# Turning the output products of a second MoE to features by tokens, and placing TensorE's operands at one offset modulo 512 bytes

## The chip, the core and the metric

The kernel runs on one core of one Trainium2 chip. The metric is the device time of one execution in microseconds (us); the median of the runs is given. Of the engines, PE is TensorE (PEld its weight loads), DVE is VectorE, ACT is ScalarE, POOL is GpSimd and SP is SyncE, which issues all transfers here.

## The reference

Three stages follow one another: linear attention with a decaying state, a gated MoE (one expert) with silu, and a second MoE (one expert) with g = h - tanh(h).

```python
for t in range(S):                                   # B, H, S, D = 4, 8, 768, 48
    cur = einsum('bhd,bhe->bhde', u * k[t], v[t])
    y[t] = einsum('bhd,bhde->bhe', r[t], state + cur)
    state = w[t][..., None] * state + einsum('bhd,bhe->bhde', k[t], v[t])
x = y as (3072 tokens, 384)
x = (silu(x @ w_gate) * (x @ w_val)) @ w_out         # d_ff 1536
h = x @ w_in                                         # d_ff 2048
return (h - tanh(h)) @ w_out2                        # (3072, 384)
```

## The kernel before

**Number format.** Activations and weights are split into a high part (rounded to fp32r) and a low part (the rest, also fp32r). Each product is three fp32r matmuls: high by high, high by low, low by high. The attention uses plain fp32 matmuls.

**Tiling.** The 3072 tokens are six blocks of TB = 512; the 384 features are KD = 3 chunks of 128. A matmul multiplies a stationary operand (128 x 128, loaded by a weight load ahead of it) with a moving one of up to 512 columns, into one PSUM bank.

**Order.** The order of the instructions is written by hand (`manual_schedule`), and each engine runs its own in program order.

1. Attention, in 24 units, is interleaved with the first half (f = 0 to 5) of the first MoE over the six blocks (`mlp`, L597): per f, nine projection matmuls for the gate, nine for the value (`proj`, L512, the matmul is L516), and nine output products (`po`, L644). The output products have the weights stationary and the 512 tokens moving, into three PSUM banks a0 to a2 (features by tokens). Attention's own matmuls are L267, L287, L304, L347 and L354.
2. Attention's pools are closed and wpb is opened in their place. The second half (f = 6 to 11) runs over the six blocks alone, one step of 27 matmuls per f. Its weights are in wpb.
3. The second MoE: per block j and m = 0 to 15 (`hm`, L835) nine projection matmuls into a bank from `ptile`; `act1` (L840) then makes z and zs on ACT, t and g on DVE and the high part hi on ACT; `act2` (L851) makes the low part lo one step later on DVE. `om` (L870) runs two steps after its `hm`: it calls `oprod` (L861), which has a slice of 128 tokens of g stationary and the 384 columns of the weight moving, for four token slices, three matmuls each (L867), into four banks. After m = 15 the four banks are copied out (L879 on DVE, L881 on ACT) and stored by SP (L883). One step is thus hm(m), then om(m - 2).
4. At the end, small sums on DVE decide (two flags) whether slow fallback paths run; for these inputs they don't.

**The second MoE's weights.** W2 has 32 tiles: the first 18 (m = 0 to 8) go to wpa, the others (m = 9 to 15) to wpb.

**Where the tiles lie.** In each SBUF partition, pools follow one another in the order in which they are opened, each tile rounded up to 32 bytes. Most tiles are multiples of 512 bytes; a few small ones shift what comes behind them. Worked out from the sizes, the byte offset modulo 512 is:

| pool, tiles | before |
|---|---|
| wpa (weights), xp (x, x2), sb (s, t, hi, lo) | 96 |
| mx, okf, fs, fi at the end of sb (32 bytes each) | 96 to 192 |
| f64, stage, ws, wpb (weights) | 224 |
| attention io: four w of 2080 bytes, then rk, rkd, v | 224 to 320, then 352 |
| attention wk: ident, cm; then rst, wmx; then SE, kT | 352; then 416 |
| attention wk: four P of 2080, e, x0; then c; then kt, A, q | then 32; then 96 |

The slices that a matmul takes are 512 bytes apart (v: 256), so they keep their tile's offset.

Of the kernel before, what the change touches and what calls it, by code (L numbers as in the profile page):

```python
# [8 lines left out]
FP32 = mybir.dt.float32  # L9
FP32R = mybir.dt.float32r  # L10
I32 = mybir.dt.int32
# [7 lines left out]
NTOK, DM = B * S, H * D  # L19
HR = 64  # L20
FF1, FF2 = 1536, 2048
NF, NM = FF1 // 128, FF2 // 128
KD = DM // 128
TB = 512
NB = NTOK // TB
HF = NF // 2
CW = 129
# [86 lines left out]
class attention:  # L114
# [3 lines left out]
    def __init__(self, nc, ctx, tc, const, ins, accw, accx):  # L118
        self.nc = nc
        self.rkw_d, self.tok_d, self.v_d, self.ub_d = ins  # L120
        self.accw, self.accx = accw, accx
        self.const = const
        PSUM = bass.MemoryType.PSUM
        self.io = ctx.enter_context(tc.tile_pool(name="io", bufs=3))
        self.wk = ctx.enter_context(tc.tile_pool(name="wk", bufs=2))
        self.ps = ctx.enter_context(tc.tile_pool(name="aps", bufs=3, space=PSUM))
        self.u = [dict() for _ in range(NU)]
        wk = self.wk
        self.u_sb = wk.tile([128, 2, 2 * 96], FP32, name="u_sb", bufs=1)
        self.ident = wk.tile([128, 128], FP32, name="ident", bufs=1)  # L130
        self.cm = wk.tile([128, 4, 128], U32, name="cm", bufs=1)
        self.rst = wk.tile([128, 4, CW], FP32, name="rst", bufs=1)
        self.wmx = wk.tile([128, 1], FP32, name="wmx", bufs=1)

        self.SE = [[[wk.tile([128, 2, 128], FP32, name=f"SE{a}{b}{c}", bufs=1) for c in range(2)]
                    for b in range(2)] for a in range(2)]
# [22 lines left out]
    def load_w(self, u):  # L159
        if u >= NU:  # L160
            return
        s = self.u[u]
        s["w"] = self.io.tile([128, 4 * CW], FP32, tag="w", name="w", bufs=4)
        self.nc.sync.dma_start(out=s["w"], in_=self.rkw_d[u, :, 1024:])

    def load_rk(self, u):
# [26 lines left out]
    def scan(self, u):  # L193
        s = self.u[u]
        w = s["w"]
        s["P"] = self.wk.tile([128, 4, CW], FP32, tag="P", name="P", bufs=4)
        fl = lambda x: x.rearrange("p a b -> p (a b)")
        self.nc.vector.tensor_tensor_scan(fl(s["P"]), w, fl(self.rst), 0.0, ALU.mult, ALU.max)  # L198
        yield
# [20 lines left out]
    def diag(self, u):  # L220
        nc, s = self.nc, self.u[u]
        r, k = s["rk"][:, 0, :], s["rk"][:, 1, :]
        nc.vector.tensor_tensor(r, r, k, ALU.mult)
        yield
        r4 = r.rearrange("p (a c e) -> p a c e", a=2, c=2)
        ub = self.u_sb[:, u % 2, :].rearrange("p (a e) -> p a e", a=2)
        nc.vector.tensor_tensor(r4, r4, ub[:, :, None, :].to_broadcast([128, 2, 2, 96]), ALU.mult)
        yield
        s["c"] = self.wk.tile([128, 8], FP32, tag="c", name="c")
        nc.vector.tensor_reduce(s["c"], r.rearrange("p (c d) -> p c d", d=D), AX.X, ALU.add)  # L230
        yield

# [243 lines left out]
def body(ctx: ExitStack, tc: tile.TileContext, rkw, tok, vtok, ub, w1, w2, rf, kf, vf, wf, uf, out):  # L476
    nc = tc.nc
    PSUM = bass.MemoryType.PSUM

    const = ctx.enter_context(tc.tile_pool(name="const", bufs=1))  # L480
# [15 lines left out]
    sa_t = const.tile([128, 1], FP32, name="sa_t")  # L496
    qa_t = const.tile([128, 1], FP32, name="qa_t")
    zsw_t = const.tile([128, 1], FP32, name="zsw_t")
    xs_d = dram.tile([NB, 128, 2, KD, TB], FP32, name="xs_d")
    pt_d = dram.tile([NB, 128, KD, TB], FP32, name="pt_d")  # L500
    w_d = dram.tile([3 * NF + 2 * NM, 128, 2, 384], FP32, name="w_d")
# [152 lines left out]
    with tc.manual_schedule():  # L654
# [53 lines left out]
        for b in range(NB):  # L708
            last = b == NB - 1
            if last:  # L710
                cb.until(3 * HF)
                pa.close()
                ex = ctx.enter_context(tc.tile_pool(name="ex", bufs=2, space=PSUM))
                wpb = ctx.enter_context(tc.tile_pool(name="wpb", bufs=3 * HF))
                pb = ExitStack()
                pin = pb.enter_context(tc.tile_pool(name="pin", bufs=2))
                x2p = pb.enter_context(tc.tile_pool(name="x2p", bufs=1))
                for i in cb.order:
                    fetch(wpb, i, W)

            def gap(f, i, b=b, last=last):
                j = 3 * f + i
                chains = [] if last else agap()
                if b == 0:
                    if j % 2:
                        chains.append(c1.chain())
                    if c1.n <= j:
                        c1.until(j)
                elif b == 1 and j == 0:
                    c1.until(3 * HF)  # L730
                    cb.loads(2)
                elif j % 4 == 2:
                    chains.append(cb.chain())
                return chains

            def done(a, b=b):
                if b == NB - 1:
                    t = pin.tile([128, KD, TB], FP32, tag="pin", name="pin")
                elif b == NB - 2:
                    t = x2p.tile([128, 2, KD, TB], FP32R, tag="x2", name="x2")[:, 0].bitcast(FP32)  # L740
                else:
                    t = pp_.tile([128, KD, TB], FP32, tag="pt", name="pt")

                def copy(k):
                    nc.scalar.copy(out=t[:, k], in_=a[k])
                    if k == KD - 1:
                        if b == NB - 1:
                            ptin[b] = t
                        else:
                            nc.sync.dma_start(out=pt_d[b], in_=t)  # L750

                for k in range(KD):
                    later(k // 2, lambda k=k: copy(k))

            if b + 1 < NB:
                nc.sync.dma_start(out=xs_d[b], in_=xt[b].bitcast(FP32))
            tail = mlp(xt[b], range(HF), tail, gap, done)
# [60 lines left out]
            tail = mlp(xt[b], range(HF, NF), tail, gap, done, after)  # L818


        NT = TB // 128
        gg, oacc = {}, {}
        ops = None

# [4 lines left out]
            return ws.tile([128, TB], FP32, tag="ws", name="g")  # L829

        def ptile(n):
            p = pgv if n % 2 else ex
            return p.tile([128, TB], FP32, tag="p", name="p_ps")

        def hm(j, m, x):  # L835
# [19 lines left out]
            gg[j, m] = (gh, gl)  # L855

        def otiles():
            return [(pac if i < 3 else ex).tile([128, TB], FP32, tag=f"a{i}", name=f"a{i}", bufs=1)
                    for i in range(NT)]

        def oprod(a4, m, gh, gl, wt=None):  # L861
            wt = W2[2 * m + 1] if wt is None else wt
            wh, wl = wt[:, 0, :], wt[:, 1, :]
            for i in range(NT):
                sl = slice(i * 128, (i + 1) * 128)
                for n, (a, c) in enumerate(((gh, wh), (gh, wl), (gl, wh))):
                    nc.tensor.matmul(  # L867
                        a4[i][:, :DM], a[:, sl], c, start=(m == 0 and n == 0), stop=(m == NM - 1 and n == 2))

        def om(j, m):  # L870
            gh, gl = gg.pop((j, m))
            if m == 0:
                oacc[j] = otiles()
            oprod(oacc[j], m, gh, gl)
            if m == NM - 1:
                for i in range(NT):
                    o = sb2.tile([128, DM], FP32, tag="o", name="o", bufs=4)
                    if j == NB - 1 and i % 2:
                        nc.vector.tensor_copy(out=o, in_=oacc[j][i][:, :DM])  # L879
                    else:  # L880
                        nc.scalar.copy(out=o, in_=oacc[j][i][:, :DM])  # L881
                    r0 = order[j] * TB + i * 128
                    nc.sync.dma_start(out=out[r0:r0 + 128, :], in_=o)  # L883
                del oacc[j]

        def check(n):
# [34 lines left out]
        act2(*prev[-1])  # L921


        mx = sb.tile([128, 4], FP32, name="mx", bufs=1)
        okf = sb.tile([128, 4], FP32, name="okf", bufs=1)
        nc.vector.tensor_reduce(mx[:, 0:1], accw, AX.X, ALU.max)
        nc.vector.tensor_reduce(mx[:, 1:2], accx, AX.X, ALU.max)
        nc.vector.tensor_reduce(mx[:, 2:3], accm, AX.X, ALU.min)
# [5 lines left out]
        om(*prev[0])  # L934
        fz = ptile(0)
        nc.tensor.matmul(fz[0:1, 0:4], ones, okf)
        fs = sb.tile([1, 2], FP32, name="fs", bufs=1)
        nc.vector.tensor_reduce(fs[:, 0:1], fz[0:1, 0:3], AX.X, ALU.add)
        nc.vector.tensor_reduce(fs[:, 1:2], fz[0:1, 0:4], AX.X, ALU.add)
        fi = sb.tile([1, 2], I32, name="fi", bufs=1)  # L940
        nc.vector.tensor_copy(out=fi, in_=fs)
        om(*prev[1])
        flag1 = nc.values_load(fi[0:1, 0:1], min_val=0, max_val=384)
# [38 lines left out]
        with tc.If(flag2 < 512):  # L982
# [3 lines left out]
            with tc.For_i(0, NB, 1) as b:  # L986
# [3 lines left out]
                for m in range(NM):  # L990
# [19 lines left out]
                    nc.scalar.copy(out=gh, in_=zt)  # L1010
                    nc.vector.tensor_tensor(gl, zt, gh.bitcast(FP32), ALU.subtract)
                    oprod(a4, m, gh, gl, wt[1])
                for i in range(NT):
                    o = sb2.tile([128, DM], FP32, tag="o", name="o", bufs=4)
                    nc.scalar.copy(out=o, in_=a4[i][:, :DM])
                    nc.sync.dma_start(out=out[bass.ds(b * TB + i * 128, 128), :], in_=o)
            fb.close()


# [57 lines left out]
        nc.sync.dma_start(out=xs_d[n], in_=xs.bitcast(FP32))  # L1077


_OUTS = [((3072, 384), 'float32')]  # L1080


def layouts(inputs):
# [68 lines left out]
```

## Time and profile before

| | us |
|---|---|
| median of 3 runs (lowest to highest) | 1029.61 (1027.26 to 1030.06) |
| the profiled execution | 1028.71 |
| its span, first to last instruction | 1026.9 |
| PE busy in the span | 973.3 |
| DVE busy | 644.1 |
| ACT busy | 508.9 |

The profile is of one execution. A row of the timeline gives the start, the time to the end of the last one, engine, line, operation, tiles and count. A matmul's own duration contains its way through the array, so matmuls overlap; the time that one costs in a stream is the difference of two starts, divided by the count. The stages are: attention with the first half of the first MoE up to 345 us, the first half's rest to 380, its second half to 610, the second MoE to 1014, then the last stores.

### The profile page before, as it was taken

Reading aid. Unit: us, or ns where it says so; the run is one execution under the profiler, and the core shown is the slowest. Engines: PE = TensorE matmul, PEld = TensorE weight load, DVE = VectorE, ACT = ScalarE, POOL = GpSimd, SP = SyncE. Lnnn points to the kernel's source line nnn. Section 1 sums busy time; section 2 is a strip of 40 time slices with the busy share of each in tenths; the row PEclk is TensorE's granted clock in tenths of the full one; section 3 lists DMA queues with packets and bytes.
Section 4 is the critical chain, followed back from the end, with each engine's and each line's share of the span. In section 5 each row is a group of like instructions: output and inputs, shape, how many; then the busy total and the mean of one; then the engine's idle time right before and its main releaser. Section 6 shows DMA issues by size and latency. Waiting matters only on the chain.

```text
span 1026.9 us, 14184 instructions
## 1 busy us (share of the span) xinstructions
PE 973.3 (95%) x5290; PEld 825.9 (80%) x5290; DVE 644.1 (63%) x1167; ACT 508.9 (50%) x1115; POOL 3.8 (0%) x16
## 2 busy tenths in 40 slices
PE   3669999999999999999999999999999999999994
PEld 2557878888888788888888878999999999999994
DVE  8999878887874424656655535555555555554442
ACT  6767776776753213323332234454454544544541
POOL 1000000000000000000000000000000000000000
PEclk8569999999999999999999999999999999999997
DMA  8566465758552662544465844353353443520001
GB/s 308 182 213 255 125 223 191 251 179 273 175 192 70 243 256 93 184 154 154 184 210 196 308 162 158 99 177 105 93 184 93 124 159 102 185 62 1 32 1 38
DMA packets 54373, 164.14 MB, mean 160 GB/s; under 512 B 6800, under 2 KB 12304, under 8 KB 51472
## 3 DMA queue, kind: packets, MB, share of 16 engines
q1 hardware_dynamic: 54288, 163.06, 46.5%
q8 instruction: 46, 0.75, 0.3%
q14 instruction: 39, 0.32, 0.1%
HBM read 122.14 MB, written 38.54 MB: 156 GB/s over the span
## 4 chain that ended last, share of the span: by engine, by line
PE 87%; DVE 8%; DMA 2%; ACT 1%; issue 1%; SPq 0%; DVEq 0%; ACTq 0%
PE p_ps L516 47%; PE a L867 19%; PE a L644 14%; PE sc_ps L287 2%; PE y_ps L354 2%; DMA w<-in_rkw_dram 1%; PE y_ps L347 1%; DVE P L198 1%; PE kv_ps L304 1%; DMA f<-in_w_dram 1%; DVE A L293 1%; DVE cvt L95 1%; PE kT_ps L267 1%; DVE w L82 1%; DVE cvt L97 0%
## 5 line engine op out<-in xcount | busy, mean ns | idle before, releaser
L516 PE MATMUL p_ps<-x,w 128*128 128x512 f32 x2160 | 533.9, 395 | 0.1
L516 PEld LDWEIGHTS p_ps<-x,w 128*128 128x128 f32 x2160 | 401.6, 188 | 87.4 <-issue 3.7
L867 PE MATMUL a<-w,hi 128*128 128x384 f32 x768 | 197.0, 337 | 0.0
L845 DVE TENSOR_TENSOR t<-p_ps,z 128x512 f32<-128x512 f32 x96 | 66.4, 692 | 168.1 <-ACT z L843 168.1
L644 PE MATMUL a<-hi,w 128*128 128x512 f32 x432 | 148.0, 397 | 0.0
L867 PEld LDWEIGHTS a<-w,hi 128*128 128x128 f32 x768 | 140.9, 188 | 8.2
L619 DVE TENSOR_TENSOR t<-s,p_ps 128x512 f32<-128x512 f32 x72 | 49.4, 686 | 147.6 <-PE p_ps L516 137.7
L867 PE MATMUL a<-w,lo 128*128 128x384 f32 x384 | 129.9, 338 | 2.3 <-DVE lo L854 2.3
L843 ACT ACTIVATE z<-p_ps 128x512 f32<-128x512 f32 x96 | 57.8, 602 | 119.4 <-PE p_ps L516 119.4
L610 ACT ACTIVATE s<-p_ps 128x512 f32<-128x512 f32 x72 | 43.0, 598 | 113.0 <-PE p_ps L516 112.9
L848 ACT CAST hi<-g 128x512 fp32r<-128x512 f32 x96 | 59.7, 622 | 77.6 <-DVE g L846 77.6
L644 PEld LDWEIGHTS a<-hi,w 128*128 128x128 f32 x432 | 81.3, 188 | 18.6
L623 ACT CAST hi<-t 128x512 fp32r<-128x512 f32 x72 | 44.7, 621 | 96.2 <-DVE t L619 95.6
L644 PE MATMUL a<-lo,w 128*128 128x512 f32 x216 | 85.0, 394 | 1.6 <-DVE lo L627 1.6
L867 PEld LDWEIGHTS a<-w,lo 128*128 128x128 f32 x384 | 72.0, 188 | 3.3 <-DVE lo L854 3.3
L846 DVE SCALAR_TENSOR_TENSOR g<-zs,t 128x512 f32<-128x512 f32 x96 | 66.5, 693 | 10.3 <-ACT zs L844 0.5
L844 ACT ACTIVATE zs<-z,sa_t 128x512 f32<-128x512 f32 x96 | 69.6, 725 | 3.1
L854 DVE TENSOR_TENSOR lo<-g,hi 128x512 fp32r<-128x512 f32 x96 | 65.6, 683 | 0.1
L627 DVE TENSOR_TENSOR lo<-t,hi 128x512 fp32r<-128x512 f32 x72 | 49.6, 689 | 19.3 <-ACT hi L623 19.3
L238 ACT ACTIVATE A<-ident,c 128x128 f32<-128x128 f32 x192 | 58.9, 400 | 2.3 <-DVE c L230 2.3
L287 PE MATMUL sc_ps<-q,kt 64*128 64x128 f32 x384 | 34.9, 316 | 24.3 <-DVE q L255 22.7
L287 PEld LDWEIGHTS sc_ps<-q,kt 64*128 64x128 f32 x384 | 29.2, 215 | 29.5 <-DVE q L255 15.3
(86 smaller groups left out, 824.3 us busy)
## 6 DMA issues: line engine op xcount, KB each, us to landing
f<-in_w_dram SPq DMA_DIRECT2D x68, 384.0 KB, 3.9
ck<-in_w_dram SPq DMA_DIRECT2D x68, 384.0 KB, 3.1
rkd<-in_rkw_dram SPq DMA_DIRECT2D x24, 512.0 KB, 4.9
w_d<-ws SPq DMA_DIRECT2D x32, 384.0 KB, 2.6
w<-w_d SPq DMA_DIRECT2D x32, 384.0 KB, 7.3
rk<-in_tok_dram SPq DMA_DIRECT2D x24, 384.0 KB, 5.5
x_d<-x SPq DMA_DIRECT2D x6, 1536.0 KB, 6.1
x<-x_d SPq DMA_DIRECT2D x6, 1536.0 KB, 7.3
```

Source lines behind the costliest of these rows:

```text
L238: self.nc.scalar.activation(out=a[:, h, i, :], in_=self.ident, func=AF.Copy, scale=s["c"][:, 2 * i + h:2 * i + h + 1])
L287: self.nc.tensor.matmul(s["sc"][h][:, i * 128:(i + 1) * 128], s["kt"][hs, i, :], s["q"][hs, i, :])
L516: nc.tensor.matmul(ps, wt[:, part, k * 128:(k + 1) * 128], x[:, xp_, k, :], start=(n == 0), stop=(n == 3 * KD - 1))
L627: nc.vector.tensor_tensor(h["l"], h["t"], h["h"].bitcast(FP32), ALU.subtract)
L644: nc.tensor.matmul(acc[0][k], a, c, start=(first and i == 0), stop=(last and i == 2))
L843: nc.scalar.activation(out=z, in_=ps, func=AF.Square, accum_out=accz[:, i:i + 1])
L844: nc.scalar.activation(out=s, in_=z, func=AF.Square, scale=C2 ** 0.5, bias=sa_t)
L845: nc.vector.tensor_tensor(hz, ps, z, ALU.mult)
L846: nc.vector.scalar_tensor_tensor(g, s, C2 * SB, hz, ALU.add, ALU.mult)
L848: nc.scalar.copy(out=gh, in_=g)
L854: nc.vector.tensor_tensor(gl, g, gh.bitcast(FP32), ALU.subtract)
L867: nc.tensor.matmul(a4[i][:, :DM], a[:, sl], c, start=(m == 0 and n == 0), stop=(m == NM - 1 and n == 2))
```

## The change

- `otiles` gives three banks a0 to a2 (as the first MoE's) instead of four; `oprod` has the weight stationary (three slices of 128 features) and g moving (512 tokens): nine matmuls of 512 columns per m instead of twelve of 384. The second of each three uses the low part of g, which was the third.
- The three banks are copied out whole (128 x 512) and stored as features by tokens; the output tensor has the shape (block, chunk, 128, 512), and the host transposes it after the launch.
- The bank that is free goes to the projections: `ex` has three buffers, and `ptile` uses five in turn.
- mx, okf, fs and fi move to `const`; attention's w, P, rst, wmx and c move to a new pool `odd` behind its other tiles. By the same sizes wpa, xp, sb, wpb, io and wk then start at 224 modulo 512, and no tile inside shifts TensorE's operands.

```diff
+        odd = self.odd = ctx.enter_context(tc.tile_pool(name="odd", bufs=2))
...
-        self.rst = wk.tile([128, 4, CW], FP32, name="rst", bufs=1)
-        self.wmx = wk.tile([128, 1], FP32, name="wmx", bufs=1)
+        self.rst = odd.tile([128, 4, CW], FP32, name="rst", bufs=1)
+        self.wmx = odd.tile([128, 1], FP32, name="wmx", bufs=1)
...
-        s["w"] = self.io.tile([128, 4 * CW], FP32, tag="w", name="w", bufs=4)
+        s["w"] = self.odd.tile([128, 4 * CW], FP32, tag="w", name="w", bufs=4)
...
-        s["P"] = self.wk.tile([128, 4, CW], FP32, tag="P", name="P", bufs=4)
+        s["P"] = self.odd.tile([128, 4, CW], FP32, tag="P", name="P", bufs=4)
...
-        s["c"] = self.wk.tile([128, 8], FP32, tag="c", name="c")
+        s["c"] = self.odd.tile([128, 8], FP32, tag="c", name="c")
...
+    mx = const.tile([128, 4], FP32, name="mx")
+    okf = const.tile([128, 4], FP32, name="okf")
+    fs = const.tile([1, 2], FP32, name="fs")
+    fi = const.tile([1, 2], I32, name="fi")
...
-                ex = ctx.enter_context(tc.tile_pool(name="ex", bufs=2, space=PSUM))
+                ex = ctx.enter_context(tc.tile_pool(name="ex", bufs=3, space=PSUM))
...
-            p = pgv if n % 2 else ex
+            p = pgv if n % 5 in (1, 3) else ex
...
         def otiles():
-            return [(pac if i < 3 else ex).tile([128, TB], FP32, tag=f"a{i}", name=f"a{i}", bufs=1)
-                    for i in range(NT)]
-
-        def oprod(a4, m, gh, gl, wt=None):
+            return [pac.tile([128, TB], FP32, tag=f"a{k}", name=f"a{k}") for k in range(KD)]
+
+        def oprod(a, m, gh, gl, wt=None):
+
             wt = W2[2 * m + 1] if wt is None else wt
-            wh, wl = wt[:, 0, :], wt[:, 1, :]
-            for i in range(NT):
-                sl = slice(i * 128, (i + 1) * 128)
-                for n, (a, c) in enumerate(((gh, wh), (gh, wl), (gl, wh))):
-                    nc.tensor.matmul(
-                        a4[i][:, :DM], a[:, sl], c, start=(m == 0 and n == 0), stop=(m == NM - 1 and n == 2))
+            for k in range(KD):
+                wh, wl = (wt[:, i, k * 128:(k + 1) * 128] for i in range(2))
+                for n, (c, g) in enumerate(((wh, gh), (wh, gl), (wl, gh))):
+                    nc.tensor.matmul(a[k], c, g, start=(m == 0 and n == 0), stop=(m == NM - 1 and n == 2))
...
-                for i in range(NT):
-                    o = sb2.tile([128, DM], FP32, tag="o", name="o", bufs=4)
-                    if j == NB - 1 and i % 2:
-                        nc.vector.tensor_copy(out=o, in_=oacc[j][i][:, :DM])
+                for k in range(KD):
+                    o = sb2.tile([128, TB], FP32, tag="o", name="o", bufs=3)
+                    if j == NB - 1 and k == 1:
+                        nc.vector.tensor_copy(out=o, in_=oacc[j][k])
                     else:
-                        nc.scalar.copy(out=o, in_=oacc[j][i][:, :DM])
-                    r0 = order[j] * TB + i * 128
-                    nc.sync.dma_start(out=out[r0:r0 + 128, :], in_=o)
+                        nc.scalar.copy(out=o, in_=oacc[j][k])
+                    nc.sync.dma_start(out=out[order[j], k], in_=o)
...
-_OUTS = [((3072, 384), 'float32')]
+_OUTS = [((NB, KD, 128, TB), 'float32')]
...
-    return got[0]
+    return _np.ascontiguousarray(got[0].transpose(0, 3, 1, 2)).reshape(NTOK, DM)
```

## Rows read from the trace of the kernel before

**Rows 1.** The page, part 1: busy us and share of the span by engine.

```profile
PE 973.3 (95%) x5290; PEld 825.9 (80%) x5290; DVE 644.1 (63%) x1167; ACT 508.9 (50%) x1115; POOL 3.8 (0%) x16
```

**Rows 2.** Windows: stretch, length, busy PE, PEld, DVE, ACT, POOL, PEclk, DMA share, GB/s.

```profile
345.50:379.50 34.00, 34.00 (x150) 27.88 (x150) 8.90 (x14) 9.60 (x17) 0.00 (x0) 1.00 0.88 336
380.00:600.00 220.00, 220.00 (x948) 178.39 (x947) 122.43 (x219) 64.51 (x110) 0.00 (x0) 1.00 0.53 188
630.00:1000.00 370.00, 370.00 (x1857) 335.55 (x1856) 207.20 (x335) 186.78 (x373) 0.00 (x0) 1.00 0.31 100
```

**Rows 3.** Timeline of PE, first MoE, weights in wpa: start, us, engine, line.

```profile
355.32 4.24 PE L516 MATMUL p_ps<-x,w 128*128 128x512 f32 x18
...
373.68 4.24 PE L516 MATMUL p_ps<-x,w 128*128 128x512 f32 x18
```

**Rows 4.** The chain that ended last, first MoE, weights in wpb.

```profile
386.21 4.19 PE p_ps L516 x18
...
599.54 4.17 PE p_ps L516 x18
```

**Rows 5.** Timeline of PE, second MoE.

```profile
622.60 1.78 PE L516 MATMUL p_ps<-x,w 128*128 128x512 f32 x7
...
702.20 2.24 PE L516 MATMUL p_ps<-x,w 128*128 128x512 f32 x9
704.28 0.51 PE L867 MATMUL a<-w,hi 128*128 128x384 f32 x2
...
706.38 2.24 PE L516 MATMUL p_ps<-x,w 128*128 128x512 f32 x9
...
999.74 2.26 PE L516 MATMUL p_ps<-x,w 128*128 128x512 f32 x9
1001.84 0.52 PE L867 MATMUL a<-w,hi 128*128 128x384 f32 x2
...
1003.95 2.25 PE L516 MATMUL p_ps<-x,w 128*128 128x512 f32 x9
```

**Rows 6.** Groups of instructions by line and form: copies out of PSUM; busy, mean ns.

```profile
L881 ACT COPY o<-a 128x384 f32<-128x384 f32 x22 | 9.0, 488 | 3.5 <-PE a L867 3.5
L745 ACT COPY pt<-a 128x512 f32<-128x512 f32 x12 | 6.6, 582 | 0.0
L879 DVE COPY o<-a 128x384 f32<-128x384 f32 x2 | 1.1, 558 | 1.3 <-PE a L867 1.3
```

**Rows 7.** DMA issues by line: KB each, median us to landing.

```profile
w_d<-ws SPq DMA_DIRECT2D x32, 384.0 KB, 2.6
...
out_dram<-o SPq DMA_DIRECT2D x24, 192.0 KB, 2.1
```

**Rows 8.** Timeline of all engines, a block's end and a step's low part.

```profile
682.15 1.62 ACT L881 COPY o<-a 128x384 f32<-128x384 f32 x4
...
683.34 0.51 PE L867 MATMUL a<-w,hi 128*128 128x384 f32 x2
...
702.88 0.68 DVE L854 TENSOR_TENSOR lo<-g,hi 128x512 fp32r<-128x512 f32 x1
```

**Rows 9.** Timeline of PE, the second MoE's start and end: waits for lo in brackets.

```profile
620.73 0.44 PE L867 MATMUL a<-w,lo 128*128 128x384 f32 x1 [1.37 <-DVE lo L854]
...
1009.11 0.44 PE L867 MATMUL a<-w,lo 128*128 128x384 f32 x1 [0.44 <-DVE lo L854]
```

**Rows 10.** Timeline of PE, attention within the first MoE.

```profile
157.01 1.09 PE L354 MATMUL y_ps<-A,v 128*64 128x128 f32 x16
158.03 2.33 PE L516 MATMUL p_ps<-x,w 128*128 128x512 f32 x9
...
160.66 2.33 PE L516 MATMUL p_ps<-x,w 128*128 128x512 f32 x9
162.93 1.16 PE L287 MATMUL sc_ps<-q,kt 64*128 64x128 f32 x16
164.02 0.50 PE L644 MATMUL a<-hi,w 128*128 128x512 f32 x1
```

More of the change, by code (lines that the diff above doesn't have):

```diff
@@ L818, in body @@
             tail = mlp(xt[b], range(HF, NF), tail, gap, done, after)
-        NT = TB // 128
         gg, oacc = {}, {}
@@ L921, in body @@
         act2(*prev[-1])
-        mx = sb.tile([128, 4], FP32, name="mx", bufs=1)
-        okf = sb.tile([128, 4], FP32, name="okf", bufs=1)
         nc.vector.tensor_reduce(mx[:, 0:1], accw, AX.X, ALU.max)
@@ L936, in body @@
         nc.tensor.matmul(fz[0:1, 0:4], ones, okf)
-        fs = sb.tile([1, 2], FP32, name="fs", bufs=1)
         nc.vector.tensor_reduce(fs[:, 0:1], fz[0:1, 0:3], AX.X, ALU.add)
         nc.vector.tensor_reduce(fs[:, 1:2], fz[0:1, 0:4], AX.X, ALU.add)
-        fi = sb.tile([1, 2], I32, name="fi", bufs=1)
         nc.vector.tensor_copy(out=fi, in_=fs)
@@ L1012, in body @@
                     oprod(a4, m, gh, gl, wt[1])
[L1013 to L1016, printed above, removed]
+                for k in range(KD):
+                    o = sb2.tile([128, TB], FP32, tag="o", name="o", bufs=3)
+                    nc.scalar.copy(out=o, in_=a4[k])
+                    nc.sync.dma_start(out=out[bass.ds(b, 1), k].rearrange("o p t -> p (o t)"), in_=o)
             fb.close()
```

## The prediction

> **What bounds the kernel now.** I read the page first: TensorE (PE) is busy 95% of the span, DVE 63% and ACT 50% [rows 1]. A mean over stages can hide a stage with another limit, so the second view is the busy time by stretches [rows 2]: PE has no gap in the second half of the first MoE (380 to 600 us) nor in the second MoE (630 to 1000 us), and its granted clock there is 1.00, the upper level of 2.4 GHz. In these stretches only two things can shorten the kernel: fewer matmuls, or a shorter time from one matmul's start to the next one's. A busy PE does not say which matmuls are slow, so the third view is PE's own timeline, from which I take differences of start times.
>
> From it come three rates for a matmul of 512 columns.
>
> - First MoE, weights from wpa: the chains of 18 projection matmuls start at 355.32 and 373.68 [rows 3]. Between them lie three steps of 27 matmuls: 18.36 us / 81 = 226.7 ns each.
> - First MoE, weights from wpb: 386.21 to 599.54 in the chain that ended last is 34 such steps [rows 4]: 213.33 / 34 = 6.274 us, or 232.4 ns a matmul. The rows between are of one kind, 6.27 or 6.28 apart.
> - Second MoE: nine projection matmuls take 704.28 - 702.20 = 2.08 us (231 ns) where m = 7 (19 steps of 4.19 behind hm(0,4) at 622.60), with weights in wpa, and 1001.84 - 999.74 = 2.10 us (233 ns) where m = 14, with weights in wpb [rows 5]. The twelve 384-column output matmuls take 2.10 to 2.11 us in either place, 175.5 ns each.
>
> What differs between the first two is named by the code: wpa lies at 96 modulo 512 bytes, as x, hi and lo do, and wpb at 224. DMA traffic is no explanation: the fast stretch is the one with 336 GB/s and a DMA share of 0.88, the slow one has 188 GB/s [rows 2]. So **equal offsets go with 226.7 ns, unequal ones with 232.4**. The second MoE at m = 7 has equal offsets and still needs 231; there every run of nine 512-column matmuls is broken by twelve of 384. I take it that matmuls and weight loads fall into a settled rhythm only where all are alike and equally placed. That is an inference: the trace has no second MoE without the break. What bears it out is that the first MoE's output products (9 of 512 columns between 18 projections) break nothing at 226.7.
>
> **Part 1: offsets, first MoE.** Tiles follow one another in the order of their pools. The four small tiles mx, okf, fs and fi (32 bytes each) leave sb and go into const: the start of wpa, x and sb moves from 96 by 128 to 224, and f64, ws and wpb stay at 224. All operands of the fp32r matmuls then lie at 224. The second half has 36 steps (six blocks, f = 6 to 11) at 6.274 us; at the settled 27 x 226.7 = 6.121 each saves 0.153, in all **-5.5 us**. DVE is busy 122 of 220 us there [rows 2] and can follow. The first half goes from 96/96 to 224/224; nothing shows what a common offset of 224 does, so its bounds are 0 and 36 x 0.153 = +5.5 us (should it not settle). I take 0, as 96 and 224 are in the trace different only from each other, and keep the other end as a rival.
>
> **Part 2: attention.** Its small tiles (w, P, rst, wmx, c) go to a pool behind the others, so kt, q, A, v, SE, kT and ident come to 224 too. Before, 16 y products with unequal offsets (A at 96, v at 352) take 158.03 - 157.01 = 1.02 us, 16 score products with equal ones (q and kt at 96) take 164.02 - 162.93 = 1.09 us [rows 10]. The unequal ones are not the slower, so I book 0. The bounds: 24 units with some three such groups of about 1 us each are an estimated 72 us, and the 2.5% that the 512-column ones lose would be 1.8 us, in either direction.
>
> **Part 3: the second MoE.** Per m, twelve output matmuls of 384 columns become nine of 512. The step of 18 matmuls is then 18 x 226.7 = 4.081 us. Before: 622.60 is the start of hm(0,4), 1003.95 that of hm(5,15), 91 steps apart [rows 5]: 381.35 / 91 = 4.191 us. Saved 0.110 x 91 = **-10.0 us**, of which (2.11 - 2.04) x 91 = 6 are the turn and 4 the projections. If they do not settle, 231 to 232.4 makes the step 4.16 to 4.18 and the gain 1 to 3 us.
>
> The start-to-start time of the Trainium skill's page "TensorE: Matmul & The Clock Gate" (section "Wait — 56ns, not 53.3ns?") is columns / 2.4 GHz + 2.5 ns: an estimate of 1.95 us for twelve of 384 and 1.94 for nine of 512, so that the turn alone would give under 1 us. The rows above, at 175.5 and 226.7 ns, lie higher than that page's 162.5 and 215.8 and decide the sum.
>
> New waits. The second matmul of an output product now needs the low part gl, where it was the third. lo is done at 702.88 + 0.68 = 703.56, its product starts at 704.28 [rows 5, 8], about 0.1 earlier after the change: some 0.8 us in hand. Three products do wait for lo today, at the stage's start and end (the two longest at 620.73 and 1009.11) [rows 9]. DVE ends those waits at the same time as before; behind them stand eight matmuls of 227 instead of ten of 175: +0.06 each, **+0.2 us**. The weights now come from W2, present long before.
>
> Evacuation. 24 copies of 384 columns (488 ns on ACT) become 18 of 512 (582, by the first MoE's copies) [rows 6]. At a block's end the four run from 682.15 for 1.62 us, and the next block's first product comes at 683.34 [rows 8]. After: a0 is free at 682.73, a1 at 683.31, a2 at 683.90; they are needed from 683.2, 683.9 and 684.6: covered by 0.5 us. Without that cover each of five boundaries would cost up to 0.6. The z behind the copies is late by some 0.4, inside the 0.8 that lo has. At the very end ACT's 582 follows the last matmul instead of DVE's 558, and 256 KB land instead of 192 KB: between 2.1 us (192 KB) and 2.6 (384 KB) [rows 7]. Together **+0.2 us**. SP issues 18 output DMAs for 24, the projections rotate over five PSUM buffers instead of four; PE waits for neither now, so both are 0.
>
> **Sum.** -5.5 - 10.0 + 0.2 + 0.2 = -15.1 us. The profiled execution took 1028.71 us, so 1013.6; the median of the runs is 1029.61, 0.9 above it, so I forecast **1014.3 us** (own range 1011 to 1017).
>
> **Rivals.**
>
> 1. *The place, not the offset, is the cause.* wpb lies at a higher address than wpa, and its matmuls could be slower for that, or for something that goes with the stage; the trace has no equal offsets in wpb that would part the two. Then part 1 gives nothing, and only the turn is left: m up to 8 save 54 x (2.11 - 2.04) = 3.8 us, the rest 42 x (2.11 - 2.09) = 0.8; with the +0.4: -4.2, so **1025.4**. For it: one stage change moves both. Against it: projections with wpa weights in the second MoE lose too. The Trainium skill's page just named says (Part 2, step 1) that the weight load has a read port of its own and steals nothing from the running matmul; by that rule offsets would not matter, and the time would be this rival's. No row here shows the ports. Chance 0.14.
> 2. *224 does not settle (slower).* If it matters where the common offset lies and 224 keeps the 232.4 of today's mixture, the first half of the first MoE pays +5.5, part 1 gives 0, part 3 91 x (4.183 - 4.191) = -0.7: with the +0.4, +5.2, so **1034.8**. It decides from a common rate of about 231.0 ns on (972 matmuls now at 226.7, 972 at 232.4 and 91 steps of 4.191 break even there). For it: 224 has no row. Against it: with weights, x, hi and lo all at 96 the rhythm settles, and 224 is one shift of all. Chance 0.07.
> 3. *The offsets do not come out as worked out, or the settled rhythm never comes in the second MoE and the first MoE gains nothing*: only 1 to 3 us remain, **1027.5**. Chance 0.06.
> 4. *Attention gains as well*, by up to a few us where the products after its interruptions (2.27 us for nine, 162.93 back to 160.66 [rows 10]) settle sooner: **1010**. Chance 0.06.
>
> **The numbers.** Forecast 0.67. A measurement of this kernel can tell 0.3% (3.1 us) from no change. Faster: forecast, rival 1 and rival 4, 0.87. Within 0.3%: rival 3 and a little of the others, 0.06. Slower: rival 2, 0.07. The range goes from rival 4's 1010 to rival 1's 1025.4: 0.87 of the chance by the cases, somewhat less with their own spread.
>
> **What would show it.** Steps of 27 matmuls at 6.12 us all through the first MoE after attention, steps of 18 at 4.08 in the second, no PE wait at the block boundaries, nine output products in 2.04 us. A first half that stays at 6.12 with a second half at 6.27 is rival 1; one that rises to 6.27 is rival 2. A PE wait for lo or for a copy inside 630 to 990 us would make part 3 wrong. A time over 1025.4 or under 1010 makes the prediction wrong.

## The result and the profile after

The changed kernel takes 1013.74 us (median of 4 runs, 1013.02 to 1014.84), the kernel before 1029.53 (of 4): a ratio of 0.9852 (95% interval 0.9839 to 0.9864), which is 15.2 us. The forecast was 1014.3. The profiled execution took 1014.84 us with a span of 1013.1.

The page, part 1, of the changed kernel:

```profile
PE 958.1 (95%) x5002; PEld 785.2 (77%) x5002; DVE 643.6 (64%) x1166; ACT 508.6 (50%) x1110; POOL 3.8 (0%) x16
```

Against [rows 1], PE issues 288 matmuls fewer and is busy 15 us less, at the same share of 95%: it still bounds the kernel, and the span shrank with its work. DVE and ACT do what they did.

The windows of the same stretches as in [rows 2], the last one shorter:

```profile
380.00:600.00 220.00, 220.00 (x973) 182.15 (x972) 123.52 (x220) 65.22 (x112) 0.00 (x0) 1.00 0.54 192
630.00:985.00 355.00, 355.00 (x1567) 293.94 (x1567) 204.10 (x330) 183.90 (x363) 0.00 (x0) 1.00 0.32 103
```

In the first, 973 matmuls where there were 948 fill the same 220 us at the same granted clock: each costs less. The chain that ended last has the steps of the first MoE's second half, which answer to [rows 4] (the projections' matmul is L523 now, that of the second MoE's output products L872):

```profile
380.96 4.08 PE p_ps L523 x18
...
595.16 4.08 PE p_ps L523 x18
```

They are 35 steps apart: 214.20 / 35 = 6.120 us, as in [rows 3] and not 6.274. The rest of the first half, whose operands moved from 96 to 224, keeps its rate; PE's timeline has

```profile
356.32 4.24 PE L523 MATMUL p_ps<-x,w 128*128 128x512 f32 x18
...
374.68 4.24 PE L523 MATMUL p_ps<-x,w 128*128 128x512 f32 x18
...
380.80 4.24 PE L523 MATMUL p_ps<-x,w 128*128 128x512 f32 x18
```

Three steps take 374.68 - 356.32 = 18.36 us, as many as in [rows 3], and the second half begins at 380.80. PE's timeline of the second MoE answers to [rows 5] and [rows 9]:

```profile
601.12 2.20 PE L523 MATMUL p_ps<-x,w 128*128 128x512 f32 x9
...
609.28 0.39 PE L872 MATMUL a<-hi,w 128*128 128x512 f32 x1
610.29 0.50 PE L872 MATMUL a<-lo,w 128*128 128x512 f32 x1 [0.62 <-DVE lo L860]
...
612.25 2.21 PE L523 MATMUL p_ps<-x,w 128*128 128x512 f32 x9
614.29 0.39 PE L872 MATMUL a<-hi,w 128*128 128x512 f32 x1
616.10 0.50 PE L872 MATMUL a<-lo,w 128*128 128x512 f32 x1 [1.42 <-DVE lo L860]
...
618.04 2.20 PE L523 MATMUL p_ps<-x,w 128*128 128x512 f32 x9
...
985.24 2.20 PE L523 MATMUL p_ps<-x,w 128*128 128x512 f32 x9
987.28 0.39 PE L872 MATMUL a<-hi,w 128*128 128x512 f32 x1
...
989.32 2.20 PE L523 MATMUL p_ps<-x,w 128*128 128x512 f32 x9
...
994.43 0.50 PE L872 MATMUL a<-lo,w 128*128 128x512 f32 x1 [0.64 <-DVE lo L860]
...
998.53 0.39 PE L872 MATMUL a<-hi,w 128*128 128x512 f32 x1
```

From hm(0,4) at 618.04 to hm(5,15) at 989.32 are 91 steps: 371.28 / 91 = 4.080 us, where there were 4.191. Nine projections and nine output products take 2.04 each. PE waits three times, for lo, at the places of [rows 9], and nowhere in between.

The stages go by the starts of matmuls. In the kernel before, PE's timeline has these rows for the start of the first MoE's second half, the start of the second MoE, its first wait and its last matmul:

```profile
379.80 4.35 PE L516 MATMUL p_ps<-x,w 128*128 128x512 f32 x18
...
605.64 2.21 PE L516 MATMUL p_ps<-x,w 128*128 128x512 f32 x9
...
613.92 0.51 PE L867 MATMUL a<-w,hi 128*128 128x384 f32 x2
614.93 0.44 PE L867 MATMUL a<-w,lo 128*128 128x384 f32 x1 [0.50 <-DVE lo L854]
...
616.77 2.24 PE L516 MATMUL p_ps<-x,w 128*128 128x512 f32 x9
...
1013.22 0.34 PE L867 MATMUL a<-w,lo 128*128 128x384 f32 x1
```

The first MoE's second half takes 601.12 - 380.80 = 220.3 us (before 605.64 - 379.80 = 225.8), the second MoE from its first projection to its last matmul 998.53 - 601.12 = 397.4 (before 1013.22 - 605.64 = 407.6): together 15.7 us less. What lies before and behind them differs between executions: in the ten profiles of whole kernels in this study the second half begins between 379.1 and 380.8 us, and 13.2 to 14.6 us pass from the last matmul's start to the end of the span; the changed kernel alone, profiled twice, has 14.6 and 13.2 there. In the two profiles compared here the changed kernel began its second half 1.0 us later and took 0.9 us more at the end, which is why they differ by 13.9 us and the medians by 15.8.

### The profile page after: what moved, and what is told of

Read it like the earlier page. It is cut to its first block, busy times and chain, and to the rows that moved or that the text cites. A ratio compares the mean times of both kernels' runs of the same rounds, so it can differ in the third digit from the quotient of the medians.

```text
span 1013.1 us, 13589 instructions
## 1 busy us (share of the span) xinstructions
PE 958.1 (95%) x5002; PEld 785.2 (77%) x5002; DVE 643.6 (64%) x1166; ACT 508.6 (50%) x1110; POOL 3.8 (0%) x16
## 4 chain that ended last, share of the span: by engine, by line
PE 85%; DVE 9%; ACT 2%; DMA 1%; issue 1%; SPq 0%; DVEq 0%; ACTq 0%
PE p_ps L523 46%; PE a L872 19%; PE a L651 14%; PE sc_ps L290 2%; PE y_ps L357 2%; DMA f<-in_w_dram 1%; PE y_ps L350 1%; PE kv_ps L307 1%; DVE A L296 1%; DVE cvt L95 1%; DVE P L201 1%; DVE w L82 1%; DVE cvt L97 1%; DVE rk L230 1%; PE kT_ps L270 0%
## 5 line engine op out<-in xcount | busy, mean ns | idle before, releaser
L523 PE MATMUL p_ps<-x,w 128*128 128x512 f32 x2160 | 526.5, 392 | 0.0
L523 PEld LDWEIGHTS p_ps<-x,w 128*128 128x128 f32 x2160 | 402.4, 188 | 88.7 <-issue 3.9
L872 PE MATMUL a<-hi,w 128*128 128x512 f32 x576 | 192.9, 389 | 0.0
L651 PE MATMUL a<-hi,w 128*128 128x512 f32 x432 | 146.8, 394 | 0.0
L872 PEld LDWEIGHTS a<-hi,w 128*128 128x128 f32 x576 | 108.1, 188 | 22.4
L872 PE MATMUL a<-lo,w 128*128 128x512 f32 x288 | 112.4, 390 | 2.7 <-DVE lo L860 2.7
L651 PEld LDWEIGHTS a<-hi,w 128*128 128x128 f32 x432 | 81.1, 188 | 17.5
L651 PE MATMUL a<-lo,w 128*128 128x512 f32 x216 | 84.3, 390 | 0.0
L872 PEld LDWEIGHTS a<-lo,w 128*128 128x128 f32 x288 | 54.0, 188 | 15.0 <-DVE lo L860 3.9
```

Source lines behind the costliest of these rows:

```text
L523: nc.tensor.matmul(ps, wt[:, part, k * 128:(k + 1) * 128], x[:, xp_, k, :], start=(n == 0), stop=(n == 3 * KD - 1))
L651: nc.tensor.matmul(acc[0][k], a, c, start=(first and i == 0), stop=(last and i == 2))
L872: nc.tensor.matmul(a[k], c, g, start=(m == 0 and n == 0), stop=(m == NM - 1 and n == 2))
```

## Experiments

**The turn alone.** The changed kernel with its small tiles where they had been, so that wpa, x, hi and lo lie at 96 and wpb at 224.

```diff
-        self.rst = odd.tile([128, 4, CW], FP32, name="rst", bufs=1)
+        self.rst = wk.tile([128, 4, CW], FP32, name="rst", bufs=1)
...
-    mx = const.tile([128, 4], FP32, name="mx")
...
+        mx = sb.tile([128, 4], FP32, name="mx", bufs=1)
```

> The changed kernel with its small tiles back where they were: the nine turned products stay, the offsets are 96 and 224 again. Theory (equal offsets settle, wherever all matmuls have 512 columns): the 36 steps of the first MoE's second half go back from 6.12 to 6.27 us (+5.5), in the second MoE m = 0 to 8 (weights in wpa, at 96 as all else) stays at 4.08 and m = 9 to 15 (weights in wpb, at 224) goes to 18 x 232.4 = 4.18 us (42 x 0.10 = +4.3): 1013.7 + 9.8 = 1023.5 us. Rival (the turn alone carries the second MoE, the offsets only the first): all second-MoE steps stay at 4.08, 1019.2 us. Rival (the place of wpb, not its offset, made it slow, and something else mended it): the steps stay as in the changed kernel, 1013.7 us.

Measured: 1023.41 us, 0.9951 (0.9934 to 0.9968) of the kernel before. PE's timeline (projections at L518), first MoE, then second:

```profile
385.38 4.35 PE L518 MATMUL p_ps<-x,w 128*128 128x512 f32 x18
...
391.65 4.35 PE L518 MATMUL p_ps<-x,w 128*128 128x512 f32 x18
...
684.10 2.20 PE L518 MATMUL p_ps<-x,w 128*128 128x512 f32 x9
...
704.50 2.20 PE L518 MATMUL p_ps<-x,w 128*128 128x512 f32 x9
708.59 2.27 PE L518 MATMUL p_ps<-x,w 128*128 128x512 f32 x9
...
725.30 2.25 PE L518 MATMUL p_ps<-x,w 128*128 128x512 f32 x9
```

The first MoE's step is 6.27 us again. In the second, five steps with weights in wpa take 20.40 us, 4.08 each; four with weights in wpb take 16.71, 4.18 each, with the same instructions. The boundary lies where the weights go from 96 to 224. The first theory's 1023.5 us lies 0.1 from the median, closer than these runs can tell (they spread over 2.9 us): in the trace the second MoE takes 402.66 us, 5.25 more than the changed kernel's 397.41, for 4.3 expected. Both rivals are off by 4 us and more.

**The offsets alone.** The kernel before, with mx, okf, fs and fi in const and attention's small tiles in a pool behind the others, all as in the change; the twelve products of 384 columns stay.

```diff
+        odd = self.odd = ctx.enter_context(tc.tile_pool(name="odd", bufs=2))
...
+    mx = const.tile([128, 4], FP32, name="mx")
```

> The kernel before with the small tiles moved and nothing else: all operands at 224, the twelve 384-column products stay. Theory: the first MoE's second half gets its 6.12 us steps (-5.5); in the second MoE the twelve products of 384 columns break the rhythm, so its step stays at 4.18 us, as it is at m = 0 to 8 in the kernel before (m = 9 to 15 gain some 0.01 each): 1023.5 us. Rival (equal offsets are enough, the number of columns does not matter): nine projections at 2.04 us, twelve products at 2.08, a step of 4.12, -6.4 more: 1017.5 us.

Measured: 1022.75 us, 0.9942 (0.9923 to 0.9962). PE's timeline (projections at L521):

```profile
386.22 4.24 PE L521 MATMUL p_ps<-x,w 128*128 128x512 f32 x18
...
392.34 4.24 PE L521 MATMUL p_ps<-x,w 128*128 128x512 f32 x18
...
692.59 2.24 PE L521 MATMUL p_ps<-x,w 128*128 128x512 f32 x9
...
726.09 2.24 PE L521 MATMUL p_ps<-x,w 128*128 128x512 f32 x9
```

The first MoE has its 6.12 us. The second, with every operand at 224, has 33.50 us for eight steps, 4.19 each: equal offsets do nothing for it while matmuls of 384 columns break the stream. By the ratios each half of the change is worth 5 to 6 us, both together 15: the rest comes only where both hold.

**All operands at 0.** 288 bytes more in const.

```diff
+    pad = const.tile([128, 72], FP32, name="pad")
```

> The changed kernel with 288 bytes more in const, so that all of TensorE's operands lie at 0 modulo 512 instead of 224. Theory (only the difference of the offsets counts): steps of 6.12 and 4.08 us as before, 1013.7 us within 1. Rival (the common offset itself counts): other steps; at the 232.4 ns of unequal offsets all three stages lose, +5.5 +5.5 +9.2, up to 1034 us; if 0 is better than 224, steps under 6.12 and 4.08.

Measured: 1013.42 us, 0.9852 (0.9835 to 0.9869). The step of the first MoE by PE's timeline (projections at L524) is 391.67 - 385.55 = 6.12:

```profile
385.55 4.24 PE L524 MATMUL p_ps<-x,w 128*128 128x512 f32 x18
...
391.67 4.24 PE L524 MATMUL p_ps<-x,w 128*128 128x512 f32 x18
```

Where the common offset lies does not matter; 224 was no special choice.

**Matmuls alone.** One execution, of streams of 63 matmuls, three moving rows and nine weight slices in turn, every one with its weight load; the tile names of the profile tell the stream (d: the stationary operand so many bytes off the moving one; c: both at one offset; n: so many columns, e with a difference of 0, u of 128; ba and bb, nine of 512 and twelve of 384 by turns with equal offsets).

```diff
+    for d in range(0, 512, 32):
+        block(f"d{d}q", 0, d, 512)
...
+    for n in (384, 256, 128):
+        block(f"n{n}e", 0, 0, n)
+        block(f"n{n}u", 0, 128, n)
```

> Matmuls alone, with nothing else on the chip but a few loads and stores: it leaves out the whole computation and stores zeros. Streams of 63 matmuls of 512 columns, the moving operand at 0 modulo 512 bytes and the stationary one at 0, 32, 64 and so on to 480; then both at one offset (32, 64, 96, 128, 224, 256, 352); then 384, 256 and 128 columns with both at 0 and with a difference of 128; then nine of 512 and twelve of 384 by turns. Theory (only equal offsets settle): 226.7 ns at a difference of 0 and at every common offset, 232 ns at a difference of 128 and about that at the other unequal ones; the stream by turns has its nine at about 230 ns, with equal offsets too. Rival (the period is 256 or 128 bytes, not 512): a difference of 256 has 226.7 ns as well. Rival (offsets do nothing and the slow steps came from engines and transfers beside TensorE): all streams at one time.

Its timeline of PE; a stream's rate is the next one's start less its own, divided by 63:

```profile
29.20 14.45 PE L506 MATMUL d0q<-mv,st 128*128 128x512 f32 x63
43.49 14.86 PE L506 MATMUL d32q<-mv,st 128*128 128x512 f32 x63
...
87.63 14.80 PE L506 MATMUL d128q<-mv,st 128*128 128x512 f32 x63
102.27 14.87 PE L506 MATMUL d160q<-mv,st 128*128 128x512 f32 x63
...
146.10 14.45 PE L506 MATMUL d256q<-mv,st 128*128 128x512 f32 x63
160.39 14.86 PE L506 MATMUL d288q<-mv,st 128*128 128x512 f32 x63
...
433.20 2.24 PE L506 MATMUL ba<-mv,st 128*128 128x512 f32 x9
435.28 2.27 PE L506 MATMUL bb<-mv,st 128*128 128x384 f32 x12
437.38 2.24 PE L506 MATMUL ba<-mv,st 128*128 128x512 f32 x9
```

| difference of the offsets, bytes | ns a matmul of 512 columns |
|---|---|
| 0 and 256 | 226.8 |
| 192 and 448 | 229.0 |
| 128 and 384 | 232.4 |
| 32, 64, 160, 224 and the same + 256 | 233.3 |
| 96 and 352 | 234.1 |

So the price is there with nothing else running: DVE, ACT and the transfers do not make it. 128 has the 232.4 of the kernel's first MoE to the digit. The seven common offsets run at 227.0 to 227.6 with their first matmuls counted in; from the fourteenth matmul on they all have 226.7, as 0 has. But the period is **256 bytes**, not 512: the rival on this point was right. By turns, nine of 512 take 2.08 us and twelve of 384 take 2.10, as at m = 7 in [rows 5], with no other engine at work; the same by turns with a difference of 128 has 2.09 to 2.10 and 2.11, as at m = 14.

Start-to-start times (ns) at the head of one stream, both operands at 64, behind one with both at 32:

```
230 224 231 236 228 232 231 227 227 226 227 227 226 ...
```

and in the stream with a difference of 128:

```
229 230 232 241 232 231 232 228 230 233 241 232 ...
```

The first needs seven matmuls until it has its 227 227 226; the second never leaves a cycle of about seven with a peak of 241. Other differences have other cycles: at 32 bytes 235 and 232 by turns, at 192 bytes 226, 229, 232.

**wpb shifted by 256.** A tile of 256 bytes ahead of wpb puts its weights at 480; all else that TensorE reads stays at 224.

```diff
+                shift = sh.tile([128, 64], FP32, name="shift")
                 wpb = ctx.enter_context(tc.tile_pool(name="wpb", bufs=3 * HF))
```

> The changed kernel with 256 bytes ahead of wpb, so that its weights lie at 480 modulo 512 bytes and all else at 224. By the streams of matmuls alone, where a difference of 256 had 226.9 ns as a difference of 0 had: no loss, steps of 6.12 and 4.08 us, the time of the changed kernel within 1 us. Rival (the period is 512 bytes, as the change has it): the first MoE's second half at 6.27 (+5.5) and m = 9 to 15 of the second at 4.18 (+4.3), +9.8 us.

Measured: 1013.56 us, 0.9852 (0.9837 to 0.9867). PE's timeline (projections at L523):

```profile
391.68 4.24 PE L523 MATMUL p_ps<-x,w 128*128 128x512 f32 x18
...
397.80 2.43 PE L523 MATMUL p_ps<-x,w 128*128 128x512 f32 x10
```

6.12 us a step with a difference of 256 in the whole kernel too. That also shows that what slowed wpb before was its offset and not its place. The change itself says the same: the 128 bytes that leave sb go to const, ahead of it, so by the sizes wpb lies in the changed kernel exactly where it lay before, and only what it is used with has moved.

**Attention's tiles back.** The changed kernel with only w, P, rst, wmx and c in their old pools.

```diff
-        s["P"] = self.odd.tile([128, 4, CW], FP32, tag="P", name="P", bufs=4)
+        s["P"] = self.wk.tile([128, 4, CW], FP32, tag="P", name="P", bufs=4)
```

> The changed kernel with only attention's small tiles (w, P, rst, wmx, c) back in their old pools, so that q, kt and A lie at 96, v and ident at 352, SE and kT at 416, while x, hi, lo and all weights stay at 224. Theory (attention's matmuls have no price for unequal offsets, as the kernel before showed): the time of the changed kernel within 1 us, the same steps of 6.12 and 4.08. Rival (attention's products pay 2.5% as those of 512 columns do): +1.8 us.

Measured: 1013.60 us, 0.9847 (0.9833 to 0.9860). The unaltered kernel beside it on the same chip, of which this was written,

> The changed kernel unaltered, as the measure for the three that run beside it on the same chip: 1013.7 us within 1.

has 1013.60 as well, 0.9851 (0.9837 to 0.9864). Moving attention's small tiles brings nothing that these runs can tell. By the period of 256 bytes most of attention's products never had unequal offsets: A and kt at 96 are 256 from v and ident at 352, one period, and q and kt are both at 96. Only the products of SE with q and of v with kT are off, by 64, and by PE's timelines these take the same in both runs: eight with SE 0.98 us, sixteen with kT 0.60. The four tiles of 32 bytes that left sb bring all that the offsets bring.

**Other widths and smaller differences, alone.** One execution again.

> Streams of 63 matmuls alone, as in the first such run (the computation is left out, zeros are stored): 512 columns with the stationary operand 4, 8, 16, 32, 128, 192 and 256 bytes off the moving one; then 480, 448, 416, 320, 288, 224 and 192 columns with a difference of 0 and of 128; then 18 matmuls of 512 with two of 448, and with two of 128, by turns. Theory (each weight load reads beside the running matmul, and only equal offsets let the two settle): 4, 8 and 16 bytes cost as 32 did, 231 to 234 ns, 256 nothing; equal offsets are 2 to 6 ns better down to 320 columns or so and make no difference below 256, where the weight load sets the time, as at 128 columns (111.7 ns either way); two matmuls of another width unsettle the next eight or so, so that 18 take 4.08 us + 0.03 to 0.05. Rival (what counts is the 32-byte line that an address falls in): 4, 8 and 16 bytes cost nothing.

The same reading of starts, three of its rows:

```profile
158.46 13.18 PE L506 MATMUL n448e<-mv,st 128*128 128x448 f32 x63
171.48 13.01 PE L506 MATMUL n448u<-mv,st 128*128 128x448 f32 x63
184.33 12.03 PE L506 MATMUL n416e<-mv,st 128*128 128x416 f32 x63
```

| columns | equal, ns | difference 128, ns |
|---|---|---|
| 512 (both alone runs) | 226.8 | 232.4 |
| 480 | 216.7 | 217.7 |
| 448 | 206.6 | 204.0 |
| 416 | 188.3 | 190.1 |
| 384 (first run) | 173.3 | 175.9 |
| 320 | 146.7 | 146.7 |
| 288 | 131.7 | 133.3 |
| 256 (first run) | 119.8 | 118.6 |
| 224, 192, 128 | 111.5, 111.5, 110.8 | 111.6, 111.7, 111.7 |

Differences of 4, 8 and 16 bytes cost 232.3, 230.7 and 233.3 ns, so the rival of the 32-byte line falls. The part on widths half failed: equal offsets are better at 512, 480, 416, 384 and 288, the same at 320, and worse at 448 and 256. The three widths under 256 take 111 to 112, so there the columns no longer set the time. With two matmuls of 448 between them, 18 of 512 took 4.10 us, with two of 128 between them 4.14, against 4.08: +0.02 and +0.06, on either side of the expected +0.03 to 0.05.

**The low part last.** The changed kernel, with the six products per m that need hi ahead of the three that need lo, except at m = 15.

```diff
+            order = [(n, k) for n in range(3) for k in range(KD)]
+            if m == NM - 1:
+                order.sort(key=lambda nk: nk[1])
+            for n, k in order:
+                i, g = ((0, gh), (1, gh), (0, gl))[n]
```

> The changed kernel with the order of each m's nine output products changed (except at m = 15): six that need the high part first, then the three that need the low part. Theory (the three waits for lo, 2.7 us of idle PE, are partly hidden by five more matmuls of 227 ns that come ahead of them, and the settled rhythm doesn't care which bank is written): of the two waits at the start of the second MoE about 1.2 us go, of the one at its end 0.5 to 0.8: 1.7 to 2.0 us less than the changed kernel, 1012.0 us; the steps stay at 4.08 us. Rival (the start is set by DVE's chain and PE only waits later): under 0.5 us. Rival (changing the bank at every matmul costs something): a step over 4.08 us; 5 ns a product would be 96 x 9 x 5 ns = 4.3 us more.

Measured: 1012.47 us, 0.9839 (0.9826 to 0.9853). Its timeline of PE, and two rows of its waits:

```profile
599.87 2.20 PE L523 MATMUL p_ps<-x,w 128*128 128x512 f32 x9
...
996.58 0.39 PE L874 MATMUL a<-lo,w 128*128 128x512 f32 x1
```

```profile
PEld a L874 <- ACT o L888: 1.5, 5, 0.3
PE a L874 <- DVE lo L860: 1.2, 1, 1.2
```

The stage takes 396.7 us, 0.7 less than 397.4 and not 1.7. Of the three waits for lo one is left, but there is a new one: at the five block boundaries the first three products now go to three banks one after another, and wait for the copies out of them. The steps between stay at 4.08, so changing the bank costs nothing in itself.

**The low part last, but by bank at a block's start.**

```diff
-            if m == NM - 1:
+            if by_bank:
                 order.sort(key=lambda nk: nk[1])
...
+            oprod(oacc[j], m, gh, gl, by_bank=m == NM - 1 or (j > 0 and m == 0))
```

> As the run with the low part last in each m, but the old order, bank by bank, at a block's first m as well (except in the first block), where the copies free the banks one after the other. Theory (the order with the low part last saved 1.1 us at the second MoE's start and 0.55 at its end, and lost about 0.9 at the five block boundaries, because its first three products write three banks within 0.7 us of the block's start and wait for the copies): from the second MoE's first projection to the last matmul 397.4 - 1.7 = 395.8 us, where the changed kernel has 397.4 and the run before 396.7; 1012.0 us in all. Rival (the loss was the change of bank at each matmul): it stays at 396.7, 1012.5 us.

Measured: 1011.88 us, 0.9824 (0.9798 to 0.9850). PE's timeline:

```profile
599.96 2.20 PE L523 MATMUL p_ps<-x,w 128*128 128x512 f32 x9
...
614.94 0.96 PE L874 MATMUL a<-lo,w 128*128 128x512 f32 x3 [1.22 <-DVE lo L860]
...
995.71 0.39 PE L874 MATMUL a<-lo,w 128*128 128x512 f32 x1
```

995.71 - 599.96 = 395.75 us, as expected. This is the fastest kernel of the study. The trace shows its 1.7 us against the change; the ratios' intervals overlap, so the times alone do not prove it.

## Why the prediction was right

**Part 1**, -5.5 us: the first MoE's second half went from 225.8 to 220.3, -5.5, by the mechanism named: offsets 96 and 224 made equal. That 0 was taken for the first half, though 224 had no row, was right: its steps still take 6.12, and the run at 0 and the streams show that no common offset is better than another. Rival 2 falls with them.

**Part 2**, 0 for attention: right, but not by the rows that it was read from. They set A and v, at 96 and 352, as unequal offsets beside q and kt as equal ones. By the period of 256 bytes that came out later, A and v are one period apart and count as equal, and the two kinds differ in shape besides; so the rows bore nothing out. That the 0 holds is shown by the run with attention's tiles back, and rival 4 falls with it.

**Part 3**, a step of 4.081: it is 4.080, and 91 steps give -10.1 for -10.0. The inference behind it, that the fast rate comes only where all are alike and equally placed, is now shown from three sides: equal offsets with the break stay at 4.19, no break with unequal offsets gives 4.18, both together 4.08; and the stream by turns shows the 2.08 and 2.10 with PE alone. The picture of it was not quite right: unequal offsets settle as well, in a slower cycle. With these steps rival 3 falls too. The split into 6 for the turn and 4 for the projections was bookkeeping, as one does not come without the other: offsets alone brought the second MoE next to nothing.

**Rival 1** had the place for the cause. The changed kernel leaves wpb where it was, the kernel with wpb at a difference of 256 nearly so, and both have steps of 6.12 us. The rival leaned on the Trainium skill's page "TensorE: Matmul & The Clock Gate" (Part 2, step 1): the weight load has a read port of its own and takes no read bandwidth from the running matmul. That the offsets then do not matter does not come out here: the same 63 matmuls, each with its weight load, take 226.8 or 232.4 ns by the difference of two addresses alone. Whether the loads take bandwidth, and what in the chip makes the difference, no run shows.

**New waits and copies.** +0.2 for three waits: the first grew by 0.1 (616.77 - 613.92 = 2.85 before, 612.25 - 609.28 = 2.97 after), the second not at all (3.75 in both); by the waits, PE's three for lo add up to 2.7 us where they were 2.3. The second longest of them before was the first, 0.50 us at 614.93, and not the one at 1009.11. The copies at block ends were covered, as worked out: no PE wait for them. The run with the low part last shows how thin that cover is: 0.5 us of it, used up by three banks in quick order, cost 0.9 us over five boundaries. +0.2 at the end cannot be checked, as that stretch alone varies by 1.4 us between two profiles of one kernel.

**The sum**: -15.1 forecast, -15.2 by the ratio, and the two large terms are each met to 0.1 us in the trace, so they do not cancel errors. Taken from the median of 1029.61 the sum gives 1014.5 and not 1014.3, a slip of 0.2.

## What to carry to other kernels

Read PE's rate from differences of start times, stage by stage, with the operands' addresses beside it: two stages of the same instructions at 6.12 and 6.27 us showed the whole cost. In long streams of 512-column fp32r matmuls, place moving and stationary operands at one offset modulo 256 bytes and keep all matmuls at one width (in this kernel each of the two alone gave 5 to 6 us of the 15); small tiles that shift an offset go to the end of the memory, and nothing needs padding to a fixed address. At other widths measure first, as at 448 and 256 columns equal offsets are the worse ones.

## What the runs showed of the hardware that was not expected

- The period is 256 bytes: differences of 0 and 256 both have 226.8 ns, and the whole kernel with wpb 256 off keeps its 6.12 us a step. Even 4 bytes of difference cost 5.5 ns.
- Unequal offsets do not keep the stream from settling; they settle it in another cycle, at a difference of 128 of about seven matmuls with one of 241 ns. How many matmuls equal offsets need to reach 227 depends on what came before: in the streams two behind two matmuls of 128 columns, three behind two of 448, three to nine at the head of a stream behind other offsets. Nine between runs of twelve with 384 columns never reached it and took 231 ns each.
- The cost is not even in the width: 448 columns take 206.6 ns with equal offsets and 204.0 with a difference of 128, and the widths of 128, 192 and 224 all take 111 to 112 ns with a weight load of 128 columns each.
- The Trainium skill's page named above (section "Wait — 56ns, not 53.3ns?") gives columns / 2.4 GHz + 2.5 ns, by which 512 columns would take an estimated 215.8 and 384 take 162.5. The best streams here, with a weight load per matmul, have 226.8 and 173.3, 11 ns more in both; the measured rates decide.
